# Two of the eight Wout pieces converted inside the last feed-forward, and block 0's products behind block 1

## The chip, the cores and the metric

The kernel runs on one core of a Trainium2 chip. The metric is the device time of one execution in microseconds; lower is better. The core has TensorE (PE, with its weight loads shown as PEld), VectorE (DVE), ScalarE (ACT), GpSimd (POOL) and SyncE (SP), whose queue issues most DMAs. Each engine works through its own instructions in order, and waits on semaphores for the others.

## The reference

Three modules follow one another: an attention with a learned relative bias, a mixture of eight experts with one expert for each token, and a plain feed-forward. All inputs are float32. What matters here is the end of the second and all of the third:

```python
for e in range(E):                      # 8 experts, D = 512, F = 1024, 2304 tokens
    mask = expert_idx == e
    h = np.maximum(x[mask] @ w1[e], 0.0)
    out[mask] = gate_w[mask, None] * (h @ w2[e])
...
h = x @ w_in                            # 2304 x 512 @ 512 x 2048
r = np.maximum(h, 0.0)
g = r * r
return (g @ w_out).astype(np.float32)   # 2304 x 2048 @ 2048 x 512
```

w_in and w_out reach the kernel as 64-bit floating point words, seen as pairs of 32-bit halves.

## The kernel before

The kernel keeps float32 accuracy with float16 matmuls: each operand is split into a high and a low float16 half, and each product is made of three matmuls (high-high, high-low, low-high).

**Expert stage.** `run_slots(0, NMOST)` goes over 22 slots of 128 tokens of one expert. In each slot PE does ff1 in two halves (2 x 48 matmuls, L1220), eight or sixteen transposes (L1203) and ff2 (24 matmuls, L1235). Four slots ahead, SP loads the next expert's first weights (`load_slot`, L999, 2 MB), and one slot ahead, between the matmuls of ff2, its second weights (`load_w2`, L1008, vt<-wsc, 2 MB); both are skipped when the expert stays the same.

**Conversion.** Into the same slots goes the conversion of the third module's weights from 64-bit words to float16 halves: `convert(i)` handles one of 16 pieces, eight of w_in (kept in `wih`) and eight of w_out. A piece's steps are a 1 MB load (L1106 or L1109), an Abs on ACT (L1116), two tensor_scalars (L1118, L1119) and two shift steps (L1121, L1123) on DVE, for w_out four subtractions of 256 columns on POOL (L1136), a cast on ACT (L1140), a subtraction on DVE (L1142) and a store of 896 KB to `wosc` in DRAM (L1144). `pieces` writes the order of these steps out by hand, with loads three pieces ahead for the first ones and two ahead for the last four. `piece(t, n)` paces them: in quarter n of slot t the generator `conv` is called until

```python
while done[0] < (1 if t < 2 else 1 + (t - 2 + 0.25 * n) * CPACE):
```

no longer holds, with CPACE = 6.1 calls a slot. The w_out product uses a 2 x 2 scheme with seven products instead of eight (Strassen's, in Winograd's form), so POOL's subtractions make the seven weight combinations.

**Last feed-forward.** It begins when the expert stage is over. SP loads all eight w_out pieces from `wosc` into `woh` (L1505). Nine blocks of 256 tokens follow. `g_unit(j, c)` is one of eight units of a block: 24 matmuls into one of four PSUM buffers `pf1` (L1422), a relu on ACT into `gf` (L1428, two buffers of a pair of units each), and after each second unit a square (L1433, on ACT for blocks 0 and 1, on DVE later), four combinations on POOL (L1438), and then, for the pair before, `g_split`: a cast on ACT (L1445) and a subtraction on DVE (L1446), which write the float16 halves `g2`. `ff2_of(j)` is a generator with the seven products of a block, each of 24 matmuls over the eight pairs c of g2 and woh (L1460), with their scalings and sums on ACT and DVE and two scatters to the output. The loop at the end places them: in block j, products of block j - 1 are called ahead of units c > 2 (c > 4 in block 1), and what is left of them behind the block's last unit.

Pools wait for the tiles whose memory they take over; the order on each engine is the order in which the program writes the instructions.

Of the kernel before, what the change touches and what calls it, by code (L numbers as in the profile page):

```python
# [7 lines left out]
F32 = mybir.dt.float32  # L8
F16 = mybir.dt.float16
U32 = mybir.dt.uint32  # L10
I32 = mybir.dt.int32
AF = mybir.ActivationFunctionType
ALU = mybir.AluOpType
# [10 lines left out]
P = 128  # L24
# [14 lines left out]
W1S, W2S, YS = 64.0, 64.0, 2.0 ** -8  # L39
WIS, RS, WOS = 64.0, 2.0 ** -8, 64.0  # L40
OUTS = 2.0 ** -22
CPACE = 6.1
NCONV, NWIN = 16, 8
HSW = 134
TINY64, HUGE = 2.0 ** -15 * 1.125, 3e38

# [37 lines left out]
def body(ctx: ExitStack, tc: tile.TileContext, q, k, v, wsm, emb, tau, mw1, mw2, win, wout, cst_d, lsk_d, ids_d, out):  # L84
    nc = tc.nc
    win, wout = win.bitcast(U32), wout.bitcast(U32)
    PE, ACT, DVE, POOL, SP = nc.tensor, nc.scalar, nc.vector, nc.gpsimd, nc.sync
# [863 lines left out]
    with tc.manual_schedule():  # L951
# [231 lines left out]
        wrp = ep("e_wr", 1)  # L1183
# [77 lines left out]
            DVE.tensor_copy(orow[:, i:i + 1], yr[:, DM + 1:XW])  # L1261


        conv = pieces([convert(i, wrp) for i in range(NCONV)])
        done = [0]
        state = ["tail"]
        yq, yd = [], []
# [115 lines left out]
        with ExitStack() as fctx:  # L1383
            fp = lambda n, bufs, **kw: tp(fctx, n, bufs, **(kw if "space" in kw else dict(side="right")))
            woh = fp("f_wo", 1).tile([P, 8, 2, 7, 256], F16, name="woh")
            gp = fp("f_g", 2)
            gfp = fp("f_gf", 2)
            op_ = fp("f_o", 2)
            up = fp("f_u", 1)
            ysp2 = fp("f_ys", 2)  # L1390
            pf1 = fp("f_p1", 4, space=PSUM)
            pf2 = fp("f_p2", 1, space=PSUM)
            NB = NTILE // 2
            gts, gfs, late, outs = {}, {}, [], []
            yv = lambda j: y0[:, :, :, 256 * (j % 2):256 * (j % 2) + 256]

            def y_load(j):
                for i in range(2):
                    t = 2 * j + i
                    SP.dma_start(out=us_t[t % 4][:, :XW], in_=y_d[t * P:(t + 1) * P, :])  # L1400

            def y_split(t):
                y2, yr = yv(t // 2), us_t[t % 4]
                y_rows(t, yr)
                ysr = ysp2.tile([P, 2, 4, P], F16, name="ysr")
                y4 = yr[:, :DM].rearrange("p (k n) -> p k n", k=4)
                o = slice(t % 2 * P, t % 2 * P + P)
                ACT.copy(ysr[:, 0], y4)
                DVE.tensor_tensor(out=ysr[:, 1], in0=y4, in1=ysr[:, 0], op=ALU.subtract)
                for a in range(2):  # L1410
                    SP.dma_start_transpose(out=y2[:, a, :, o], in_=ysr[:, a].rearrange("p k n -> p (k n)"))

            def g_unit(j, c):
                y2 = yv(j)
                if c == 0:
                    gts[j] = gp.tile([P, 2, 7, 8, P], F16, name="g2")
                p_ = pf1.tile([P, 2, 256], F32, name="pf1")
                for h in range(2):
                    f, i = 8 * h + c, 0
                    for kc in range(4):  # L1420
                        for a, b in ((0, 0), (0, 1), (1, 0)):
                            PE.matmul(p_[:, h], lhsT=wih[:, a, kc, f * P:(f + 1) * P], rhs=y2[:, b, kc, :],  # L1422
                                      start=(i == 0), stop=(i == 11))
                            i += 1
                if c % 2 == 0:
                    gfs[j] = gfp.tile([P, 8, 2, P], F32, name="gf")
                g = gfs[j]
                ACT.activation(g[:, 0:4, c % 2, :], p_.rearrange("p h (i n) -> p (h i) n", i=2), AF.Relu, scale=RS)  # L1428
                if c % 2 == 0:
                    return  # L1430
                g4 = g[:, 0:4].rearrange("p q c n -> p (q c n)")
                if j < 2:
                    ACT.activation(g4, g4, AF.Square)  # L1433
                else:
                    DVE.tensor_tensor(out=g4, in0=g4, in1=g4, op=ALU.mult)  # L1435
                for d, x, y, op in ((4, 0, 2, ALU.add), (5, 4, 1, ALU.subtract), (6, 1, 0, ALU.subtract),
                                    (7, 3, 5, ALU.subtract)):
                    POOL.tensor_tensor(out=g[:, d], in0=g[:, x], in1=g[:, y], op=op)  # L1438
                g_split()
                late.append((g, gts[j], c - 1))  # L1440

            def g_split():
                while late:
                    g, gt, c = late.pop()
                    ACT.copy(gt[:, 0, :, c:c + 2, :], g[:, 1:8])  # L1445
                    DVE.tensor_tensor(out=gt[:, 1, :, c:c + 2, :], in0=g[:, 1:8], in1=gt[:, 0, :, c:c + 2, :], op=ALU.subtract)  # L1446

            def ff2_of(j):
                gt = gts.pop(j)
                m = [meta[:, 2 * j + i, 0:1] for i in range(2)]  # L1450
                bank = [pf2.tile([P, 512], F32, name=f"pf2_{x}")[:, :256] for x in "abcd"]
                pa, pb, pc, pd = bank
                o = [op_.tile([P, DM], F32, name=f"o{i}") for i in range(2)]
                u = lambda nm: up.tile([P, 256], F32, name=nm)

                def prod(ps, s, w, first, end):
                    i = 0
                    for c in range(8):
                        for a, b in ((0, 0), (0, 1), (1, 0)):
                            PE.matmul(ps, lhsT=gt[:, a, s, c, :], rhs=woh[:, c, b, w, :],  # L1460
                                      start=(i == 0 and first), stop=(i == 23 and end), skip_group_check=True)
                            i += 1

                def comb(dst, ps, i, x):
                    DVE.scalar_tensor_tensor(out=dst, in0=ps, scalar=m[i], in1=x, op0=ALU.mult, op1=ALU.add)

                def put(i):
                    t = 2 * j + i
                    w = POOL.indirect_dma_start(out=out, out_offset=bass.IndirectOffsetOnAxis(ap=orow[:, t:t + 1], axis=0),  # L1469
                                                in_=o[i], in_offset=None, bounds_check=NT - 1, oob_is_err=False).ins  # L1470
                    for other in outs:
                        tc.declare_no_dep(w, other, reason="disjoint rows")
                    outs.append(w)

                prod(pa, 0, 0, True, False)
                s = [u(f"s{i}") for i in range(2)]
                for i in range(2):
                    ACT.activation(s[i], pa, AF.Copy, scale=m[i])
                yield
                prod(pb, 4, 4, True, True)  # L1480
                u2 = [u(f"u{i}") for i in range(2)]
                for i in range(2):
                    comb(u2[i], pb, i, s[i])
                yield
                prod(pc, 3, 3, True, False)
                u4 = u("u4")
                comb(u4, pc, 0, u2[0])
                yield
                prod(pd, 5, 5, True, False)
                comb(o[0][:, 256:], pd, 0, u4)  # L1490
                yield
                prod(pa, 2, 2, False, True)
                ACT.activation(o[1][:, :256], pa, AF.Copy, scale=m[1])  # L1493
                yield
                prod(pc, 6, 1, False, True)
                comb(o[1][:, 256:], pc, 1, u2[1])
                put(1)
                yield
                prod(pd, 1, 6, False, True)
                comb(o[0][:, :256], pd, 0, u2[0])  # L1500
                put(0)
                yield

            for g in range(8):
                SP.dma_start(out=woh[:, g].rearrange("p a q n -> p (a q n)"), in_=wosc[:, g * 3584:(g + 1) * 3584])  # L1505
            for j in range(NB):
                two = ff2_of(j - 1) if j else iter(())
                last = j == NB - 1
                for c in range(8):
                    if c > (2 if j > 1 else 4) and not (last and c == 6):  # L1510
                        next(two, None)
                    g_unit(j, c)
                    if 0 < j < NB - 1:
                        if c == 0:
                            y_load(j + 1)
                        if c in (3, 5):
                            y_split(2 * (j + 1) + c // 2 - 1)
                if last:
                    g_split()
                for _ in two:  # L1520
                    pass
            for _ in ff2_of(NB - 1):
                pass
# [66 lines left out]
```

## Time and the profile before

| what | value |
|---|---|
| median of 3 runs | 1011.57 us (1011.03 to 1012.91) |
| profiled execution | 1017.84 us, span 1016.0 us |
| PE busy in the span | 947.2 us (93%) |
| DVE, ACT, POOL busy | 662.3, 540.9, 497.0 us |
| granted PE clock, mean | 0.982 |
| expert stage, first to last ff2 | 404 to 648 us |
| last feed-forward | 650 to 1005 us |

The span runs from the first to the last instruction of the profiled execution; what is outside it (1.8 us) is start and end. Busy time of an engine is the time in which it executes an instruction; idle time is put down to what released the engine.

### The profile page before, as it was taken

Reading aid. Unit: us, or ns where it says so; the run is one execution under the profiler, and the core shown is the slowest. Engines: PE = TensorE matmul, PEld = TensorE weight load, DVE = VectorE, ACT = ScalarE, POOL = GpSimd, SP = SyncE. Lnnn points to the kernel's source line nnn. Section 1 sums busy time; section 2 is a strip of 40 time slices with the busy share of each in tenths; the row PEclk is TensorE's granted clock in tenths of the full one; section 3 lists DMA queues with packets and bytes.
Section 4 is the critical chain, followed back from the end, with each engine's and each line's share of the span. In section 5 each row is a group of like instructions: output and inputs, shape, how many; then the busy total and the mean of one; then the engine's idle time right before and its main releaser. Section 6 shows DMA issues by size and latency. Waiting matters only on the chain. (4 is left out here: it accounts for less than half of the span.)

```text
span 1016.0 us, 24944 instructions
## 1 busy us (share of the span) xinstructions
PE 947.2 (93%) x9725; PEld 749.5 (74%) x9725; DVE 662.3 (65%) x1229; ACT 540.9 (53%) x1000; POOL 497.0 (49%) x415
## 2 busy tenths in 40 slices
PE   8687999999899879999989999999999999999995
PEld 4456776677577658777657667688888888888884
DVE  6665999988988664677866867245445455545441
ACT  6666777777777574455756665255323333333330
POOL 1213536437433352456637787266454554645541
PEclk9798999999999999999999999999999999999998
DMA  9988985998779343698898574362111111111001
GB/s 299 329 242 265 327 276 174 303 267 265 242 228 326 137 125 108 229 336 300 336 410 318 196 271 170 143 275 50 25 53 43 32 52 43 32 53 22 22 1 42
DMA packets 78844, 187.18 MB, mean 184 GB/s; under 512 B 26648, under 2 KB 26776, under 8 KB 76128
## 3 DMA queue, kind: packets, MB, share of 16 engines
q1 hardware_dynamic: 72656, 169.98, 50.1%
q0 software_dynamic: 6064, 15.54, 4.6%
q8 instruction: 78, 1.28, 0.6%
q14 instruction: 46, 0.38, 0.1%
HBM read 171.65 MB, written 51.73 MB: 220 GB/s over the span
## 5 line engine op out<-in xcount | busy, mean ns | idle before, releaser
L1438 POOL TENSOR_TENSOR gf<-gf 128x256 f32<-128x256 f32 x144 | 165.9, 1171 | 146.5 <-DVE gf L1435 124.5
L1422 PE MATMUL pf<-big,wih 128*128 128x256 f16 x1728 | 196.0, 273 | 1.7 <-PEq L1376 1.7
L1422 PEld LDWEIGHTS <-wih 128*128 128x128 f16 x1728 | 169.0, 98 | 21.6 <-issue 2.1
L1460 PEld LDWEIGHTS <-g 128*128 128x128 f16 x1512 | 147.4, 98 | 18.7 <-issue 1.0
L1428 ACT ACTIVATE gf<-pf 128x512 f32<-128x512 f32 x72 | 42.5, 597 | 193.5 <-PE pf L1422 135.7
L1220 PE MATMUL ph<-x,w1b 128*128 128x128 f16 x2112 | 125.6, 219 | 4.6 <-ACT x L1204 2.4
L1220 PEld LDWEIGHTS <-w1b 128*128 128x128 f16 x2112 | 120.6, 98 | 9.5 <-issue 4.4
L471 POOL TENSOR_TENSOR wh<-wr,w2s_c 128x1024 f16<-128x1024 f32 x32 | 61.4, 1918 | 132.4 <-DMA wr<-in_mw_dram 83.1
L1235 PE MATMUL py<-vt,h 128*128 128x512 f16 x528 | 119.0, 382 | 6.1 <-DMA vt<-wsc 6.1
L1446 DVE TENSOR_TENSOR g<-gf,g 128x1792 f16<-128x1792 f32 x36 | 85.5, 2375 | 50.2 <-ACT g L1445 50.2
L522 ACT ACTIVATE pr<-ssb,mn 128x576 f32<-128x576 f32 x144 | 111.8, 777 | 11.9 <-DVE mn L509 11.7
L509 DVE CUSTOM_DVE_ANT_0 ssb<-ps_s,bias 128x576 f32<-128x576 f32 x144 | 107.5, 749 | 4.6 <-DMA bias<-bias_d 2.5
L498 PE MATMUL ps_s<-kst,qd 128*128 128x288 f16 (+1 forms) x640 | 96.4, 291 | 14.0 <-DVE mn L509 9.5
L1435 DVE TENSOR_TENSOR gf<-gf 128x1024 f32<-128x1024 f32 x28 | 34.3, 1225 | 113.6 <-ACT gf L1428 113.6
L1235 PEld LDWEIGHTS <-h 128*128 128x128 f16 x528 | 51.1, 98 | 65.0 <-issue 8.6
L531 PE MATMUL ps_t<-cst,pr 128*128 128x128 f32 x576 | 92.7, 284 | 1.3 <-DVE pt L209 0.6
L556 PE MATMUL pv<-pt,vt 128*64 128x128 f32 (+1 forms) x1280 | 85.1, 276 | 8.0 <-DMA vt<-in_v_dram 5.7
L556 PEld LDWEIGHTS pv<-pt,vt 128*64 128x64 f32 x1280 | 67.6, 141 | 24.4 <-issue 18.2
L531 PEld LDWEIGHTS ps_t<-cst,pr 128*128 128x128 f32 x576 | 65.3, 145 | 24.8 <-issue 19.7
L498 PEld LDWEIGHTS <-qd 128*128 128x128 f16 (+1 forms) x640 | 56.4, 101 | 29.1 <-issue 18.5
L207 ACT COPY pt<-ps_t 128x512 f32<-128x512 f32 x99 | 57.1, 577 | 14.9 <-PE ps_t L531 11.0
L1445 ACT CAST g<-gf 128x1792 f16<-128x1792 f32 x36 | 60.3, 1676 | 4.3 <-POOL gf L1438 4.3
(194 smaller groups left out, 1547.8 us busy)
## 6 DMA issues: line engine op xcount, KB each, us to landing
vt<-wsc SPq DMA_DIRECT2D x88, 512.0 KB
wr<-in_mw_dram SPq DMA_DIRECT2D x76, 512.0 KB
kst<-in_mw_dram SPq DMA_DIRECT2D x44, 512.0 KB
wsc<-wh SPq DMA_DIRECT2D x32, 512.0 KB
bias<-bias_d SPq DMA_DIRECT2D x16, 576.0 KB
bias_d<-rt SPq DMA_DIRECT2D x28, 295.5 KB
qd<-qh SPq DMA_DIRECT2D x64, 128.0 KB
wr<-in_win_dram SPq DMA_DIRECT2D x8, 1024.0 KB
```

The source lines that it names most:

```text
L471: POOL.tensor_tensor(out=wh[:, 0], in0=wr, in1=w2s_c.to_broadcast([P, 1024]), op=ALU.mult)
L498: PE.matmul(s[r, hf, :288], lhsT=qd[:, h2, i, pr, r], rhs=kst[x - x % 2][:, pr, h2, x % 2, js], start=(i == 0), stop=(i == 1))
L509: DVE.tensor_tensor_reduce(out=ss.rearrange("p (a j) -> p a j", a=2), in0=s[:, :, :288], in1=btile[bkey[u]][:, h2].rearrange("p (a j) -> p ...
L522: ACT.activation(pr_sb[k_ // 2][:, h2], ssb.pop(k_), AF.Exp, bias=mns.pop(k_), scale=-1.0, accum_out=sums[c, b][:, h:h + 1])
L531: PE.transpose(pt_ps[k_][:, jc * P:(jc + 1) * P], src[:, j0:j0 + P], eye)
L556: PE.matmul(pv[o, cs], lhsT=vb[:, 2 * jc + h2, d] if jc < 4 else vb[o, 8, d], rhs=a[h2][:, jc, cs] if jc < 4 else e[o, cs], start=(jc == 0 ...
L1220: PE.matmul(p_[:, f4, :], lhsT=w[:, a, kc, f * P:(f + 1) * P], rhs=x2[:, b, kc, :], start=(i == 0), stop=(i == 11))
L1235: PE.matmul(p_, lhsT=h2[:, a, fc, :], rhs=wb2[fc // 2][:, b, fc % 2, :], start=(i == 0), stop=(i == 23))
L1422: PE.matmul(p_[:, h], lhsT=wih[:, a, kc, f * P:(f + 1) * P], rhs=y2[:, b, kc, :], start=(i == 0), stop=(i == 11))
L1438: POOL.tensor_tensor(out=g[:, d], in0=g[:, x], in1=g[:, y], op=op)
L1446: DVE.tensor_tensor(out=gt[:, 1, :, c:c + 2, :], in0=g[:, 1:8], in1=gt[:, 0, :, c:c + 2, :], op=ALU.subtract)
L1460: PE.matmul(ps, lhsT=gt[:, a, s, c, :], rhs=woh[:, c, b, w, :], start=(i == 0 and first), stop=(i == 23 and end), skip_group_check=True)
```

## The change

Only 14 of the 16 pieces are converted in the expert stage, at 5.4 calls a slot. The raw rows of the last two w_out pieces are loaded at the start of the last feed-forward into the memory of block 1's `g2` tile, before that tile gets its own contents. `finish(i)` does the same steps on them as `convert` (its scratch lies in that tile too) and writes the halves straight into `woh[:, 6]` and `woh[:, 7]`. The dictionary `ORDER` says after which units (8 j + c) of blocks 0 and 1 each next step is emitted. The six other pieces come from `wosc` as before. g2's dimensions are put in another order, so that a pair of units fills one contiguous quarter of the tile. Block 0's seven products no longer stand between units of block 1, but all behind its last unit.

```diff
-CPACE = 6.1
-NCONV, NWIN = 16, 8
+CPACE = 5.4
+NCONV, NWIN, NLATE = 16, 8, 2
...
-        conv = pieces([convert(i, wrp) for i in range(NCONV)])
+        conv = pieces([convert(i, wrp) for i in range(NCONV - NLATE)])
...
-                if c == 0:
-                    gts[j] = gp.tile([P, 2, 7, 8, P], F16, name="g2")
+                if c == 0 and j not in gts:
+                    gts[j] = gp.tile([P, 4, 2, 7, 2, P], F16, name="g2")
...
-                    ACT.copy(gt[:, 0, :, c:c + 2, :], g[:, 1:8])
-                    DVE.tensor_tensor(out=gt[:, 1, :, c:c + 2, :], in0=g[:, 1:8], in1=gt[:, 0, :, c:c + 2, :], op=ALU.subtract)
+                    ACT.copy(gt[:, c // 2, 0], g[:, 1:8])
+                    DVE.tensor_tensor(out=gt[:, c // 2, 1], in0=g[:, 1:8], in1=gt[:, c // 2, 0], op=ALU.subtract)
...
-                            PE.matmul(ps, lhsT=gt[:, a, s, c, :], rhs=woh[:, c, b, w, :],
+                            PE.matmul(ps, lhsT=gt[:, c // 2, a, s, c % 2, :], rhs=woh[:, c, b, w, :],
...
-            for g in range(8):
+            for j in range(2):
+                gts[j] = gp.tile([P, 4, 2, 7, 2, P], F16, name="g2")
+            spare = gts[1].rearrange("p d a q c n -> p (d a q c n)").bitcast(U32)
+            rows = [spare[:, :2048], spare[:, 3072:5120]]
+            flat = spare[:, 5120:7168].bitcast(F32)
+            bits = [spare[:, 6144:7168], spare[:, 2048:3072]]
+            for i in range(NLATE):
+                g = 8 - NLATE + i
+                SP.dma_start(out=rows[i], in_=wout[g * P:(g + 1) * P, :])
+
+            def finish(i):
+                wr = rows[i].rearrange("p (n t) -> p n t", t=2)
+                lo, hi = wr[:, :, 0], wr[:, :, 1]
+                tb = flat.rearrange("p (q n) -> p q n", q=8)
+                af, b = flat[:, :1024], bits[i]
+                bf = b.bitcast(F32)
+                ACT.activation(bf, hi.bitcast(F32), AF.Abs)
+                yield
+                DVE.tensor_scalar(bf, bf, TINY64, None, op0=ALU.max)
+                DVE.tensor_scalar(b, b, 3, 0x3FFFFFF8, op0=ALU.logical_shift_left, op1=ALU.bitwise_and)
+                yield
+                DVE.scalar_tensor_tensor(out=b, in0=lo, scalar=29, in1=b, op0=ALU.logical_shift_right, op1=ALU.bitwise_or)
+                yield
+                DVE.scalar_tensor_tensor(out=af.bitcast(U32), in0=hi, scalar=0xC0000000, in1=b,
+                                         op0=ALU.bitwise_and, op1=ALU.bitwise_or)
+                yield
+                for d, x, y in ((4, 0, 1), (5, 2, 4), (6, 2, 0), (7, 3, 5)):
+                    POOL.tensor_tensor(out=tb[:, d], in0=tb[:, x], in1=tb[:, y], op=ALU.subtract)
+                yield
+                dh, dl = (woh[:, 8 - NLATE + i, a].rearrange("p q n -> p (q n)") for a in range(2))
+                ACT.activation(dh, flat[:, 256:], AF.Copy, scale=WOS)
+                yield
+                DVE.scalar_tensor_tensor(out=dl, in0=flat[:, 256:], scalar=WOS, in1=dh, op0=ALU.mult, op1=ALU.subtract)
+                yield
+
+            ends = [finish(i) for i in range(NLATE)]
+            ORDER = {3: (0,), 4: (0,), 5: (0, 0), 6: (0, 1), 7: (1,), 8: (0, 1), 9: (0,), 10: (1, 1), 12: (1,), 13: (1,)}
+
+            for g in range(8 - NLATE):
...
-                    if c > (2 if j > 1 else 4) and not (last and c == 6):
+                    if j > 1 and c > 2 and not (last and c == 6):
                         next(two, None)
                     g_unit(j, c)
+                    for i in ORDER.get(8 * j + c, ()):
+                        next(ends[i])
```

## Rows read from the trace of the kernel before

**Rows 1.** Windows, two stages: start and end, busy us of each engine (instructions), clock, DMA.

```profile
404.06:649.98 245.92, 234.65 (x2639) 169.56 (x2636) 175.30 (x237) 139.18 (x173) 154.44 (x138) 0.99 0.75 278
649.98:1004.60 354.62, 353.82 (x3240) 316.35 (x3240) 166.81 (x159) 126.41 (x157) 183.51 (x162) 1.00 0.19 56
```

**Rows 2.** PE's waits, 404 to 650 us: us in total, times, longest.

```profile
PE py L1235 <- DMA vt<-wsc: 6.1, 3, 3.4
...
PE ph L1220 <- ACT x L1204: 1.3, 2, 1.0
...
PE ph L1220 <- DVE w1b L1015: 1.0, 2, 0.6
```

**Rows 3.** PE in order of time, expert stage: start, us, operation, idle before.

```profile
485.25 5.34 PE L1235 MATMUL py<-vt,h 128*128 128x512 f16 x24 [2.42 <-DMA vt<-wsc]
...
522.24 6.75 PE L1235 MATMUL py<-vt,h 128*128 128x512 f16 x24 [3.39 <-DMA vt<-wsc]
```

**Rows 4.** Window of the expert stage, up to slot 10's product.

```profile
508.00:522.00 14.00, 10.53 (x126) 7.80 (x124) 9.48 (x11) 9.16 (x13) 7.99 (x8) 0.99 1.02 413
```

**Rows 5.** SP's queue in order of time, slot 9.

```profile
506.99 0.41 SPq L1109 DMA_DIRECT2D wr<-in_wout_dram  x1
508.71 4.69 SPq L1008 DMA_DIRECT2D vt<-wsc  x4
```

**Rows 6.** Groups by line, 404 to 650 us: the conversion's steps (busy us, mean ns).

```profile
L1136 POOL TENSOR_TENSOR tb<-tb 128x256 f32<-128x256 f32 x32 | 26.1, 835 | 12.9 <-DVE tb L1123 6.3 <-DVE ys L1244 5.9
...
L1121 DVE SCALAR_TENSOR_TENSOR tb<-wr,tb 128x1024 uint32<-128x1024 uint32 x16 | 20.0, 1252 | 1.1 <-DVEq L1024 0.8 <-DMA vt<-wsc 0.2
...
L1116 ACT ACTIVATE tb<-wr 128x1024 f32<-128x1024 f32 x16 | 18.5, 1157 | 17.3 <-DVE wr L1142 6.9 <-DVE wih L1131 3.9 <-issue 3.4
L1142 DVE SCALAR_TENSOR_TENSOR wr<-tb,wr 128x1792 f16<-128x1792 f32 x8 | 16.1, 2018 | 5.1 <-ACT wr L1140 5.1
...
L1140 ACT ACTIVATE wr<-tb 128x1792 f16<-128x1792 f32 x8 | 13.6, 1695 | 11.5 <-POOL tb L1136 10.8 <-DVE tb L1119 0.7
...
L1118 DVE TENSOR_SCALAR tb<-tb 128x1024 f32<-128x1024 f32 x16 | 13.0, 815 | 2.3 <-DVEq L1024 2.0
```

**Rows 7.** ACT in order of time, blocks 0 and 1.

```profile
673.05 1.08 ACT L1428 ACTIVATE gf<-pf 128x512 f32<-128x512 f32 x2 [2.69 <-DVE g L1446]
...
681.58 1.67 ACT L1445 CAST g<-gf 128x1792 f16<-128x1792 f32 x1
685.94 1.08 ACT L1428 ACTIVATE gf<-pf 128x512 f32<-128x512 f32 x2 [2.69 <-DVE g L1446]
```

**Rows 8.** PE in order of time, blocks 0 and 1.

```profile
649.98 34.22 PE L1422 MATMUL pf<-big,wih 128*128 128x256 f16 x312 [1.66 <-PEq L1376]
684.03 2.78 PE L1460 MATMUL pf_a<-woh,g 128*128 128x256 f16 x24
686.65 2.78 PE L1422 MATMUL pf<-big,wih 128*128 128x256 f16 x24
...
710.23 5.95 PE L1422 MATMUL pf<-big,wih 128*128 128x256 f16 x53
```

**Rows 9.** POOL in order of time, blocks 0 and 1.

```profile
657.19 2.89 POOL L1438 TENSOR_TENSOR gf<-gf 128x256 f32<-128x256 f32 x4 [5.55 <-ACT gf L1433]
...
675.30 4.68 POOL L1438 TENSOR_TENSOR gf<-gf 128x256 f32<-128x256 f32 x4 [1.76 <-ACT gf L1433]
```

**Rows 10.** DVE in order of time, blocks 0 and 1.

```profile
676.83 2.57 DVE L1446 TENSOR_TENSOR g<-gf,g 128x1792 f16<-128x1792 f32 x1 [3.88 <-ACT g L1445]
...
696.89 2.57 DVE L1446 TENSOR_TENSOR g<-gf,g 128x1792 f16<-128x1792 f32 x1 [3.33 <-ACT g L1445]
```

**Rows 11.** SP's queue at the start of the last feed-forward.

```profile
656.45 5.62 SPq L1505 DMA_DIRECT2D woh<-wosc  x8
```

**Rows 12.** Windows around slot 10's product.

```profile
519.00:520.00 1.00, 0.00 (x0) 0.00 (x0) 0.69 (x1) 1.00 (x2) 0.00 (x0) 1.00 1.04 393
522.00:525.00 3.00, 2.77 (x7) 1.01 (x7) 2.75 (x4) 1.19 (x2) 1.97 (x2) 0.50 1.02 410
```

## The prediction

> **What bounds the kernel now.** I read the busy times by stage first [rows 1]. The reader is to see two stages that are both filled by TensorE: the expert stage, 245.9 us with 234.7 us of it busy, and the last feed-forward, 354.6 us with 353.8 us busy. In the second there is nothing to win: its PE work is 9 blocks of 15 groups of 24 matmuls, and only lost PE time can change its length. In the first, the waits of PE say what could be won [rows 2]: 6.1 us for the loads of the second expert weights (vt<-wsc), 2.3 us for ACT and DVE (1.3 and 1.0); in the order of time the two large ones are 2.42 us ahead of slot 7's product and 3.39 us ahead of slot 10's, and that last product then ran 6.75 us where slot 7's took 5.34 [rows 3], 1.4 us more. So all gaps of the stage that loads and conversion could cause are 6.1 + 2.3 + 1.4 = 9.8 us.
>
> **Part 1, the pace (16 pieces at 6.1 become 14 at 5.4).** In the 14 us up to slot 10's product the DMA engines are 102% busy and move 413 GB/s [rows 4]: here the transfers set the pace, and each MB ahead of slot 10's weights makes them later by 1.05 MB / 413 GB/s = 2.5 us. A call number k of the conversion runs in the first quarter slot above 2 + (k - 2)/CPACE. The load of piece 9 is call 45: 43/6.1 = 7.05 puts it into slot 9.25, and the queue view shows it at 506.99, just ahead of slot 10's weights at 508.71 [rows 5]. With 5.4, 43/5.4 = 7.96, it goes to slot 10.0, behind them. Of five loads (calls 17, 24, 31, 38, 45) four stay ahead: 2.5 us of the 3.39 go, and about 0.9 is left, less than the 2.42 after which the clock stayed up [rows 3], so the 1.4 us go too. The load of piece 6 moves the other way, from slot 5.75 (ahead of slot 9's raw weights) to 6.25 (behind them, ahead of slot 7's second weights): the 2.42 us can grow by the head start that is lost (I take 2 us, about the time of its own 1 MB, less than the 2.5 us above), but what is lost there is transferred in the meantime, so that the sum up to slot 10 stays. Of the 2.3 us behind ACT and DVE I take a third, 0.8, since a slot has 11% fewer steps. Gain 2.5 + 1.4 + 0.8 = 4.7 us; bounds: a loss of 1 us (piece 6 costs 2 that come back only in part), and all of 9.8.
>
> **Part 2, the conversion inside blocks 0 and 1.** Two pieces bring, each, an ACT Abs (1.16), two DVE tensor_scalars (0.81 for the first), two DVE shift steps (1.25 each), four POOL subtractions (0.84 each), an ACT cast (1.70) and a last DVE subtraction (2.02) [rows 6]. The sums would fit in the idle time of the three engines; the question is what stands behind each step in its queue. Now the elementwise work of a pair of units is a chain: two relus, square, cast of the pair before, subtraction of the pair before, and only then the next relus, because there are two gf buffers. It takes 6.45 us a pair (two pairs from 673.05 to 685.94 [rows 7]) where PE needs 2 x 2.62 = 5.24 (684.03 to 686.65 [rows 8]). PE does not feel that yet: four PSUM buffers let it run ahead, and unit 14 would need unit 10's relu (685.94 + 0.6) when PE comes to it at 649.98 + 14 x 2.62 = 686.7. There is no slack left at that point even without conversion. POOL has little room too: its four operations of a pair take 2.89 us alone and 4.68 us beside a DVE subtraction of 2.57 [rows 9, 10].
>
> Into this chain go, by the written order: the Abs of the second piece between relus 6 and 7, which run back to back (+1.16); the cast of the first piece between relus 8 and 9 (+1.70); and the first piece's POOL work ahead of pair 3's. It starts when DVE has done two shift steps behind the subtraction that ends at 672.95 (676.83 - 3.88 [rows 10]), at 675.5, and runs until about 679.7 (2.9 alone, 4.7 beside DVE); pair 3's four then last until about 685.3, beside 2.9 us of DVE steps, where its cast would have come at 681.58 + 1.16 + 1.70 = 684.4: +0.9. Together the chain is 3.7 us late: relu 10 begins at about 689.6, unit 14 at 690.2 instead of 686.7, unit 15 ends at about 695.5.
>
> The end of the second piece decides. DVE's last step of piece one and the second shift step of piece two follow the subtraction of pair 3 at 689.6: 691.8, 693.0. Piece two's POOL work stands beside pair 4's subtraction and the split of y: 5.9 us, to 698.9. ACT has relu 12 at 696.1 and then waits for it: cast to 700.6, relu 13 and square to 702.2, cast of pair 5 to 703.9, subtraction of pair 5 to 706.4, and behind that, in DVE's queue, piece two's last subtraction, to 708.8.
>
> **Part 3, block 0's products behind block 1.** Now three of seven lie between units, from 684.03 on, and block 2 begins at 710.23 [rows 8]. The order alone costs PE nothing: 16 units and 7 products end at 710.2 either way. But the first product goes through all eight weight pieces, and its 23rd matmul reads the low half of piece 8. Without a wait it would run at 649.98 + 16 x 2.62 + 22 x 0.109 = 694.3; by part 2 it waits until 708.8. The loss is 14.5 us (the 3.5 us ahead of unit 14 lie inside it, since the end of the chain sets the resume). Bounds: were the chain not lengthened at all, the last step would still follow the subtraction that now ends at 696.89 + 2.57 = 699.46 [rows 10] and end at 701.5, a loss of 7.2; were the raw rows some 4 us late as well, because their loads come as late as the woh loads do now (656.45 [rows 11]) and share the engines with them, and POOL stretched by 2 us more, it would be 715, a loss of 20.7. I take 14.5, since the 6.45 us chain of now fits the same stretched durations.
>
> **The clock.** After 3.39 us without a matmul the granted clock went from 1.00 to 0.50, that is 2.4 to 1.2 GHz, and stayed there for 2.8 us after the restart at 522.24 [rows 12]; this was worth 1.4 us [rows 3]. A wait of 11 us in block 0's first product should do that too: +1.4, once. The Trainium skill, page "TensorE: Matmul & The Clock Gate", section "Part 1: The HAM clock gate", says the same in general: the slow clock is the default, and sustained activity releases it. The trace agrees at slot 10; by that rule the sum is the one below, and without it 1.4 us less.
>
> **Part 4, what costs nothing.** Two direct loads of 1 MB replace two round trips through wosc; they are issued at the start of the stage, and the DMA share there leaves room (0.19 over the stage [rows 1]). The new order of g2's dimensions keeps every operand's size. The steps' scratch lies in g2 of block 1, whose first quarter is written only at unit 11, after the first piece's raw rows were read. If that cover fails, it is the upper bound above.
>
> **Sum.** -4.7 + 14.5 + 1.4 = +11.2 us. The profiled execution took 1017.8 us (span 1016.0), 6.3 more than the median of the runs, 1011.6; I put the difference on the median: 1022.8 us.
>
> **Rivals.** (a) The chain keeps its pace: the steps fall into idle time (ACT 2.69, DVE 3.88, POOL 1.76 us a pair [rows 7, 9, 10]), and only the last subtraction's place costs: 7.2 + 1.4 - 4.7 = +3.9, 1015.5 us. For it: the sums fit. Against: Abs and cast stand between relus that run back to back. (b) Faster: with the products gone from the queues the chain runs ahead of now (relu 13 no longer waits behind two scalings), and piece two ends at 698.0: loss 3.7, no clock fall worth counting, -4.7 + 3.7 = -1.0, or 1010.6; it decides from an end before 699.0. Against: now's own subtraction of pair 5 ends at 699.46, and the last step is queued behind it. (c) Dearer: late rows and a second fall of the clock, 20.7 + 2.8 - 4.7 = +18.8, 1030.4, and up to 1036 if the expert stage gives nothing. (d) The expert stage gives all 9.8: with 15.9 in the other stage still +6.1, 1017.7; it lies inside my range.
>
> **How the numbers follow.** Forecast, with (d), 0.62, own range 1016 to 1029; (a) 0.12; (c) 0.10; (b) 0.11; about no change 0.05 (the measurement tells 0.2%, 2 us, from none). Leaving out the outer part of (c) and most of (b), the range is 1011 to 1030. Faster 0.11, same 0.05, slower 0.62 + 0.12 + 0.10 = 0.84.
>
> **What would show it.** Right: in block 0's first product a PE wait of 8 to 13 us, released by DVE's last subtraction of the second piece (or ACT's cast just before), a half-speed clock behind it, 2 to 4 us ahead of unit 14 released by ACT; in the expert stage less waiting for vt<-wsc, above all at slot 10. Wrong: PE without a gap between 650 and 725; a wait of ACT's Abs for the rows; or an expert stage as long as before or longer.

## The result and the profile after

The changed kernel takes 1021.71 us (median of 10 runs, 1014.77 to 1025.69) against 1011.63 us of the kernel before on the same chip (10 runs): ratio 1.008, 95% interval 1.0054 to 1.0106. It is slower by about 0.8%, some 8 to 10 us; the prediction was 1022.8 us. The profiled execution of the changed kernel took 1024.84 us, 7.0 more than that of the kernel before.

The profile says where. From the first matmul of slot 0's ff2 to the first matmul of the last feed-forward the changed kernel needs 640.53 - 403.58 = 236.95 us, the kernel before 245.92 [rows 1]: 9.0 us less. From there to the first matmul of block 2 it needs 717.30 - 640.53 = 76.77 us, the kernel before 710.23 - 649.98 = 60.25 [rows 8]: 16.5 us more. From there to the start of the last product both need the same 291.85 us (717.30 to 1009.15 and 710.23 to 1002.08).

PE of the changed kernel in order of time, blocks 0 and 1 (start, us, operation, idle before and what ended it); it answers to [rows 8]:

```profile
640.53 36.84 PE L1422 MATMUL pf<-big,wih 128*128 128x256 f16 x336 [0.43 <-PEq L1376]
680.64 6.88 PE L1422 MATMUL pf<-big,wih 128*128 128x256 f16 x48 [3.27 <-ACT gf L1428]
687.36 2.46 PE L1460 MATMUL pf_a<-woh,g 128*128 128x256 f16 x21
690.50 0.27 PE L1460 MATMUL pf_a<-woh,g 128*128 128x256 f16 x1 [0.69 <-ACT woh L1534]
698.71 0.58 PE L1460 MATMUL pf_a<-woh,g 128*128 128x256 f16 x2 [7.94 <-DVE woh L1536]
699.09 5.28 PE L1460 MATMUL pf_b<-woh,g 128*128 128x256 f16 x24
...
717.30 8.02 PE L1422 MATMUL pf<-big,wih 128*128 128x256 f16 x72
```

The 16 units run as one stretch up to unit 13; ahead of unit 14 PE stands 3.27 us for a relu. Block 0's first product gets through 21 matmuls, waits 0.69 us for the high half of the last weight piece, piece 8, and 7.94 us for its low half, and the product behind the wait takes 5.28 us instead of 2.78. Units 14 and 15 took 6.88 us instead of 5.40 (48 matmuls). The clock is the reason for both long ones; windows of the changed kernel (start and end, length, busy us of PE, PEld, DVE, ACT, POOL, then PE clock, DMA share, GB/s):

```profile
680.00:682.00 2.00, 1.36 (x7) 0.96 (x7) 2.00 (x1) 1.97 (x3) 0.48 (x1) 0.57 0.00 0
682.00:684.00 2.00, 2.00 (x13) 1.42 (x12) 1.81 (x3) 2.00 (x3) 0.30 (x1) 0.57 0.00 0
...
694.00:698.00 4.00, 0.00 (x0) 0.00 (x0) 4.00 (x2) 1.80 (x4) 2.77 (x2) 0.50 0.17 33
699.00:702.00 3.00, 3.00 (x16) 2.07 (x15) 2.88 (x4) 1.77 (x3) 2.92 (x3) 0.50 0.23 44
```

It is at or near its lower level, 1.2 GHz, after each of the two gaps. ACT in order of time, answering to [rows 7]:

```profile
663.62 0.60 ACT L1428 ACTIVATE gf<-pf 128x512 f32<-128x512 f32 x1 [2.70 <-DVE g L1446]
664.12 1.16 ACT L1520 ACTIVATE g<-g 128x1024 f32<-128x1024 f32 x1
665.18 0.58 ACT L1428 ACTIVATE gf<-pf 128x512 f32<-128x512 f32 x1
...
675.88 1.69 ACT L1445 CAST g<-gf 128x1792 f16<-128x1792 f32 x1 [1.35 <-POOL gf L1438]
...
688.75 1.70 ACT L1534 ACTIVATE woh<-g 128x1792 f16<-128x1792 f32 x1 [1.75 <-POOL g L1531]
```

The two late pieces, the seventh and eighth of w_out, are called piece 7 and piece 8 from here on. Abs of piece 8 stands between relus 6 and 7 (663.62 and 665.18). The cast of pair 3 at 675.88 had waited 1.35 us for POOL, and the cast of piece 8 at 688.75 had waited 1.75 us for POOL; both waits are in the forecast. POOL's rows, answering to [rows 9]:

```profile
659.43 4.69 POOL L1438 TENSOR_TENSOR gf<-gf 128x256 f32<-128x256 f32 x4 [1.76 <-ACT gf L1433]
666.53 4.69 POOL L1531 TENSOR_TENSOR g<-g 128x256 f32<-128x256 f32 x4 [2.42 <-DVE g L1527]
671.18 9.30 POOL L1438 TENSOR_TENSOR gf<-gf 128x256 f32<-128x256 f32 x8
683.70 5.02 POOL L1531 TENSOR_TENSOR g<-g 128x256 f32<-128x256 f32 x4 [3.22 <-DVE g L1527]
688.68 2.90 POOL L1438 TENSOR_TENSOR gf<-gf 128x256 f32<-128x256 f32 x4
```

From 666.53 to 680.48 POOL is never idle: four subtractions of piece 7 (4.69 us) and then the eight operations of pairs 3 and 4 (9.30). And DVE's, answering to [rows 10]:

```profile
693.63 2.56 DVE L1446 TENSOR_TENSOR g<-gf,g 128x1792 f16<-128x1792 f32 x1 [5.50 <-ACT g L1445]
696.12 2.54 DVE L1536 SCALAR_TENSOR_TENSOR woh<-g,woh 128x1792 f16<-128x1792 f32 x1
```

The last step of piece 8 stands behind the subtraction of pair 5 and ends at 698.66; PE goes on at 698.71.

In the expert stage the two waits of [rows 3] look like this in the changed kernel:

```profile
480.91 1.46 PE L1235 MATMUL py<-vt,h 128*128 128x512 f16 x6 [0.26 <-DMA vt<-wsc]
482.52 4.04 PE L1235 MATMUL py<-vt,h 128*128 128x512 f16 x18 [0.16 <-DMA vt<-wsc]
...
516.73 6.87 PE L1235 MATMUL py<-vt,h 128*128 128x512 f16 x24 [2.39 <-DMA vt<-wsc]
```

Slot 7's product waits 0.42 us instead of 2.42, slot 10's 2.39 instead of 3.39, and slot 10's still runs at the low clock (6.87 us). PE's other waits of [rows 2], 1.3 us for ACT and 1.0 us for DVE, are gone.

### The profile page after: what moved, and what is told of

Its sections match the earlier page's. It is cut to its first block, busy times and chain, and to the rows that moved or that the text cites. A ratio compares the mean times of both kernels' runs of the same rounds, so it can differ in the third digit from the quotient of the medians.

```text
span 1023.1 us, 24938 instructions
## 1 busy us (share of the span) xinstructions
PE 949.2 (93%) x9725; PEld 750.8 (73%) x9725; DVE 657.3 (64%) x1229; ACT 542.1 (53%) x1000; POOL 500.2 (49%) x415
## 5 line engine op out<-in xcount | busy, mean ns | idle before, releaser
L1445 ACT CAST g<-gf 128x1792 f16<-128x1792 f32 x36 | 60.3, 1676 | 5.7 <-POOL gf L1438 5.7
```

## The experiments

All ratios are against the kernel before on the same chip in the same series, with their 95% intervals; between series the chip differs (the kernel before had medians of 1020.1, 1015.0, 1018.5 and 1018.1 us in the four), so runs of different series are compared by the lengths of their stages. These come from one profile each, "expert" from the first ff2 matmul to the first matmul of the last feed-forward, "blocks 0, 1" from there to block 2's first matmul. In single profiles the expert stage of one and the same code differs: with 14 pieces at 5.4 it took 235.2 to 240.2 us in nine of them, so a difference of a few us between two profiles of that stage proves little by itself. The three with the loads and steps of 6.1 calls (kernel before, runs 1 and 3) lie closer, 245.4 to 245.9.

| run | ratio | expert, us | blocks 0, 1, us |
|---|---|---|---|
| kernel before | 1 | 245.9 | 60.3 |
| changed kernel | 1.0080 (1.0054 to 1.0106) | 237.0 | 76.8 |
| the same again, with the third series | 1.0098 (1.0063 to 1.0133) | 239.5 | 75.6 |
| 1 order of block 0's products alone | 1.0011 (0.9976 to 1.0045) | 245.7 | 61.7 |
| 2 14 pieces at 5.4, two left out | 0.9926 (0.9892 to 0.9960) | 238.6 | 60.3 |
| 3 14 pieces at 6.1, two left out | 0.9984 (0.9952 to 1.0015) | 245.4 | 60.3 |
| 4 changed, ACT's steps moved | 1.0129 (1.0077 to 1.0181) | 240.2 | 75.8 |
| 5 changed, piece 8 last | 0.9963 (0.9927 to 0.9999) | 237.9 | 69.6 |
| 6 changed, subtractions on DVE, new order | 0.9962 (0.9931 to 0.9993) | 238.3 | 67.2 |
| 7 both of 5 and 6 | 0.9938 (0.9905 to 0.9971) | 235.2 | 64.6 |
| 8 before, loads two calls later | 0.9959 (0.9926 to 0.9993) | 242.8 | 60.6 |
| 9 one late piece | 1.0039 (1.0007 to 1.0070) | 252.1 | 61.1 |
| 10 changed, subtractions on DVE alone | 1.0102 (1.0057 to 1.0147) | 237.9 | 77.7 |
| 11 run 7, scalings first | 1.0014 (0.9983 to 1.0045) | 238.2 | 66.8 |

### 1. The order of block 0's products alone

```diff
-                    if c > (2 if j > 1 else 4) and not (last and c == 6):
+                    if j > 1 and c > 2 and not (last and c == 6):
```

> The kernel before, with one part of the change alone: all seven products of block 0 behind the last unit of block 1; nothing of the conversion is moved. Theory (the order costs nothing, the wait for the last weight piece does): same time as before within 0.2%, 0 us; in blocks 0 and 1 PE has no gap over 0.5 us, because relu 10 ends at 686.55 in the profile before and unit 14 comes at 686.7. Rival (the units run too far ahead of the elementwise chain once no products lie between them): a gap of 2 us or more ahead of unit 14 or 15, released by ACT, and some 2 to 4 us more.

Same time, within the noise. PE in order of time, in this kernel:

```profile
652.63 42.08 PE L1422 MATMUL pf<-big,wih 128*128 128x256 f16 x384 [1.12 <-PEq L1376]
...
706.01 2.78 PE L1460 MATMUL pf_a<-woh,g 128*128 128x256 f16 x24 [0.82 <-ACT s L1478]
709.05 2.78 PE L1460 MATMUL pf_c<-woh,g 128*128 128x256 f16 x24 [0.26 <-DVE u L1465]
```

All 16 units run without a gap. There are 0.82 us and 0.26 us of waiting later, for block 0's own scalings and sums, which now follow the cast and subtraction of pair 6. The first of them is over the 0.5 us that was expected. The rival, a gap ahead of unit 14 or 15, is out, with 1.4 us more in blocks 0 and 1 than before (61.7 against 60.3) as what the order does cost.

### 2 and 3. The expert stage alone, at both paces

The kernel before with 14 pieces in the expert stage; pieces 7 and 8 of Wout are not converted, and pieces 1 and 2 are loaded in their place (run 3 has the same edit with CPACE left at 6.1):

```diff
-CPACE = 6.1
+CPACE = 5.4
...
-        conv = pieces([convert(i, wrp) for i in range(NCONV)])
+        conv = pieces([convert(i, wrp) for i in range(NCONV - NLATE)])
...
-                SP.dma_start(out=woh[:, g].rearrange("p a q n -> p (a q n)"), in_=wosc[:, g * 3584:(g + 1) * 3584])
+                SP.dma_start(out=woh[:, g].rearrange("p a q n -> p (a q n)"), in_=wosc[:, g % 6 * 3584:(g % 6 + 1) * 3584])
```

> The kernel before with 14 pieces at 5.4 calls a slot and nothing else: two of the eight Wout pieces are not converted at all, and in their place woh gets pieces 0 and 1 a second time, so the output is not the reference's. It measures what the expert stage alone gains. The profile after shows 9.0 us less from slot 0's ff2 to the first matmul of the last feed-forward (236.95 against 245.92); the prediction had 4.7. Theory: 5 to 9 us faster, waits for vt<-wsc well under the 6.1 us of before. Rival (the 9.0 us are mostly a difference between two executions, not of the change): 0 to 2 us faster.

> As the run with 14 pieces in the expert stage alone (two Wout pieces left out, pieces 0 and 1 loaded twice), but at the old 6.1 calls a slot: every load of the first twelve pieces keeps its slot, and the conversion ends about two and a half slots earlier. Theory (the gain comes from loads that move behind slot 10's weights, by the slower pace): the waits for vt<-wsc stay at 5 to 6 us and the half-speed product at slot 10 stays, gain 0 to 3 us. Rival (fewer bytes and steps as such give the gain): as fast as the 5.4 run within 2 us.

14 pieces at 5.4 are 0.74% faster (7.5 us), 14 pieces at 6.1 are not faster beyond the noise. So removing two pieces at the old pace gives nothing that can be measured; going to 5.4 as well does. The slower pace moves both the loads and the other steps, and these two runs do not part them. PE's waits in the expert stage of the run at 5.4 (us in total, times, longest):

```profile
PE py L1235 <- DMA vt<-wsc: 2.5, 2, 1.6
PE ph L1220 <- issue: 2.4, 6, 0.5
```

and of the run at 6.1:

```profile
PE py L1235 <- DMA vt<-wsc: 4.8, 2, 3.0
PE ph L1220 <- ACT x L1204: 2.0, 2, 1.0
PE px L1203 <- POOL xs L1038: 1.5, 3, 0.7
...
PE ph L1220 <- DVE w1b L1015: 1.0, 2, 0.6
```

At 6.1 the weights are late by 4.8 us, and ACT, POOL and DVE hold PE for 2.0 + 1.5 + 1.0 us more; at 5.4 the first is halved and the others are gone. The theory that only loads matter is too narrow: 2.3 us of the 6.9 between the two stages are theirs. Nor did the half-speed product at slot 10 stay at 6.1, as the theory had it; in run 3 that product waited 1.72 us and took 5.60:

```profile
525.75 5.60 PE L1235 MATMUL py<-vt,h 128*128 128x512 f16 x24 [1.72 <-DMA vt<-wsc]
```

In run 1, whose expert stage is that of the kernel before, it waited 1.22 + 0.28 us. The 3.39 us of [rows 3] are what one execution showed.

### 4. ACT's steps out from between back-to-back relus

```diff
-            ORDER = {3: (0,), 4: (0,), 5: (0, 0), 6: (0, 1), 7: (1,), 8: (0, 1), 9: (0,), 10: (1, 1), 12: (1,), 13: (1,)}
+            ORDER = {3: (0,), 4: (0,), 5: (0, 0, 1), 6: (0,), 7: (1,), 8: (1,), 9: (0, 0), 10: (1, 1), 13: (1, 1)}
```

> The changed kernel with another written order of the same conversion steps: ACT's Abs of the second piece behind unit 5 and both casts behind units 9 and 13, where ACT waits for DVE's subtraction anyway, and no ACT step between two relus that run back to back. Theory (steps between back-to-back relus lengthen the chain): the gap of 3.27 us ahead of unit 14 falls below 0.7, DVE's last subtraction of the second piece ends 3 to 5 us earlier, counted from the first matmul of the stage, and the wait of block 0's first product, 8.6 us now, stays above 5 because that step still stands behind the subtraction of pair 5; time 3 to 5 us under the changed kernel, about 1017. Rival (POOL's doubled work, not ACT, holds the chain): the gap ahead of unit 14 stays at 2 us or more and the time within 1 us of the changed kernel.

The theory falls. The ratio is not below that of the changed kernel (1.0129 against 1.0080 and 1.0098, with overlapping intervals), and the gap ahead of unit 14 is what it was, on PE:

```profile
683.01 7.07 PE L1422 MATMUL pf<-big,wih 128*128 128x256 f16 x48 [3.27 <-ACT gf L1428]
```

because on ACT the cast of pair 3 now waits 3.65 us for POOL and starts as late as before, 678.24 - 642.90 = 35.34 us after the stage's first matmul (675.88 - 640.53 = 35.35 in the changed kernel):

```profile
678.24 1.69 ACT L1445 CAST g<-gf 128x1792 f16<-128x1792 f32 x1 [3.65 <-POOL gf L1438]
```

### 10 and 6. POOL's subtractions on DVE, alone and with a new order

Run 10 has the first edit, run 6 both:

```diff
-                    POOL.tensor_tensor(out=tb[:, d], in0=tb[:, x], in1=tb[:, y], op=ALU.subtract)
+                    DVE.tensor_tensor(out=tb[:, d], in0=tb[:, x], in1=tb[:, y], op=ALU.subtract)
...
-            ORDER = {3: (0,), 4: (0,), 5: (0, 0), 6: (0, 1), 7: (1,), 8: (0, 1), 9: (0,), 10: (1, 1), 12: (1,), 13: (1,)}
+            ORDER = {3: (0,), 4: (0, 0), 5: (1,), 6: (0, 0), 7: (0,), 8: (0, 1), 10: (1, 1, 1), 11: (1,), 12: (1,)}
```

> The changed kernel with one edit: the four subtractions of each late piece on DVE instead of POOL, the written order of the steps as it is. If POOL alone lengthens the chain, the gap of 3.27 us ahead of unit 14 falls below 0.7, as in the run with both edits (0.60). If the chain is as late as the later of two delays, POOL's second load or ACT's 1.16 + 1.70 us between back-to-back relus, taking one away leaves the other: 2 to 3 us stay. Moving ACT's steps alone had left 3.27.

> The changed kernel with the four subtractions of a late piece on DVE instead of POOL, and the steps written so that each stands where its engine waits: no ACT step between back-to-back relus, the last step of the second piece behind unit 12, ahead of the subtraction of pair 5. New theory after the run with the steps moved on ACT alone (POOL's second load, not ACT's, holds the chain): the cast of pair 3 no longer waits for POOL for over 1 us, the gap ahead of unit 14 falls from 3.27 to 1 us or less, and the wait for piece 8 from 8.6 to 4 to 6; 4 to 7 us under the changed kernel, 1 to 4 above the kernel before. Rival (any step more in this stretch lengthens the chain by its own time, whichever engine does it): the gap stays at 3 us.

Alone, the move leaves a gap of 2.62 us ahead of unit 14 (and 0.74 ahead of unit 12):

```profile
675.68 5.40 PE L1422 MATMUL pf<-big,wih 128*128 128x256 f16 x48 [0.74 <-ACT gf L1428]
683.71 7.07 PE L1422 MATMUL pf<-big,wih 128*128 128x256 f16 x48 [2.62 <-ACT gf L1428]
...
702.52 0.59 PE L1460 MATMUL pf_a<-woh,g 128*128 128x256 f16 x2 [7.94 <-DVE woh L1536]
```

Run 10 does not show ACT's steps alone, though, because the subtractions now delay DVE. The cast of pair 2 ended at 671.23, but its subtraction on DVE began only at 672.40, behind those of piece 7:

```profile
669.30 3.18 DVE L1531 TENSOR_TENSOR g<-g 128x256 f32<-128x256 f32 x4
672.40 2.54 DVE L1446 TENSOR_TENSOR g<-gf,g 128x1792 f16<-128x1792 f32 x1
```

So 1.2 us of the chain's delay there are DVE's new load. The rest, 2.62 + 0.74 - 1.2 = 2.2 us, is an estimate of what ACT's steps would hold alone.

With both edits, 0.60 us are left, and the wait for piece 8's low half is 2.90 instead of 7.94, less than the 4 to 6 expected:

```profile
674.89 5.40 PE L1422 MATMUL pf<-big,wih 128*128 128x256 f16 x48 [0.60 <-ACT gf L1428]
...
685.90 0.59 PE L1460 MATMUL pf_a<-woh,g 128*128 128x256 f16 x2 [2.90 <-DVE woh L1536]
```

So POOL's second load holds the chain by 3.3 us by itself (run 4), and beside it, not on top of it, stand ACT's steps between relus with some 2 us. Taking away either leaves a gap; run 6, which takes away both, closes most of it. Its new order also moves DVE's steps of both pieces, so the 0.60 is the work of the whole order and not of two edits alone. That the last step of piece 8 now stands ahead of pair 5's subtraction shortens the wait for it further.

### 5 and 7. Piece 8 last in block 0's first four products

```diff
-                def prod(ps, s, w, first, end):
-                    i = 0
-                    for c in range(8):
+                def prod(ps, s, w, first, end, cs=range(8)):
+                    i = 3 * cs[0]
+                    for c in cs:
...
-                prod(pa, 0, 0, True, False)
+                cs = range(8)
+                if j == 0:
+                    for ps, x, end in ((pa, 0, False), (pb, 4, True), (pc, 3, False), (pd, 5, False)):
+                        prod(ps, x, x, True, end, range(7))
+                    cs = range(7, 8)
+                prod(pa, 0, 0, True, False, cs)
...
```

The first calls for pb, pc and pd get the same `cs`.

> The changed kernel, in block 0's products alone: the first four of them run over weight pieces 1 to 7 first, and their matmuls on piece 8 follow behind all four. Theory (of the 16.5 us lost in the last feed-forward most is the wait for piece 8 and the slow clock behind it): 3 x 21 matmuls of 0.109 us, 6.9 us, cover the 8.6 us wait, about 1.7 us of it stay, and the half-speed stretch behind it goes; from the first matmul of the stage to block 2's first unit 8 to 10 us less than the 76.8 of the changed kernel, time equal to the kernel before within 2 us. Rival (something else behind the wait holds block 0's products, the sums on ACT and DVE): the gap comes back further on, less than 4 us won.

> Both edits together: the late pieces' subtractions on DVE in the new order, and block 0's first four products with piece 8 last. Theory: the wait for piece 8 is covered wholly (6.9 us of cover against 4 to 6), the gap ahead of unit 14 is 1 us or less, so the last feed-forward is as long as before within 1.5 us and the whole gain of the expert stage is left, 0.993 of the kernel before (the run with 14 pieces alone had 0.9926). Rival: the two edits win the same time twice, and the sum stays at 0.998 or above.

In run 5, on the changed kernel, blocks 0 and 1 are 7.2 us shorter (69.6 against 76.8), a little less than expected. The wait shrinks to 2.12 us, but the clock falls here too (0.50 granted from 701.00 to 703.00), and one product takes 4.20 us:

```profile
699.13 0.38 PE L1460 MATMUL pf_a<-woh,g 128*128 128x256 f16 x2 [2.12 <-DVE woh L1541]
...
701.24 4.20 PE L1460 MATMUL pf_a<-woh,g 128*128 128x256 f16 x24 [0.75 <-ACT s L1483]
```

In run 7 there is no wait for piece 8 any more, but one of 2.99 us for the scalings of the first product, which stand in ACT's queue behind the cast of pair 6:

```profile
674.21 5.40 PE L1422 MATMUL pf<-big,wih 128*128 128x256 f16 x48 [0.60 <-ACT gf L1428]
...
693.09 2.78 PE L1460 MATMUL pf_a<-woh,g 128*128 128x256 f16 x24 [2.99 <-ACT s L1483]
```

So blocks 0 and 1 take 4.3 us more than before, not 1.5 as expected, and the ratio, 0.9938, is still the lowest of the versions that do all the work, though its interval overlaps those of runs 5, 6 and 8.

### 11. The scalings ahead of the cast

Run 7 with the first product's scalings written ahead of pair 6's cast and subtraction.

> The fastest version so far (two late pieces with their subtractions on DVE and steps where engines wait, piece 8 last in block 0's first products), with ACT's two scalings of block 0's first product ahead of the cast of pair 6 instead of behind it. In that version PE waits 2.99 us for these scalings. Theory: the wait falls below 0.5 us, the last feed-forward is within 1.5 us of the kernel before, and the time 0.990 to 0.993 of it. Rival (DVE's sums, next in the queue behind pair 6's subtraction, hold the products instead): the wait moves to DVE u, and the time stays at 0.994.

```profile
697.84 2.78 PE L1461 MATMUL pf_a<-woh,g 128*128 128x256 f16 x24 [1.42 <-ACT s L1484]
703.15 4.27 PE L1461 MATMUL pf_c<-woh,g 128*128 128x256 f16 x24 [2.54 <-DVE u L1466]
```

The rival's mechanism holds: 1.42 us for the scalings stay, 2.54 us for DVE's sums come, and the product behind them ran at the low clock (4.27 us). It won nothing: blocks 0 and 1 take 66.8 us against 64.6, and the ratio is 1.0014, not the 0.994 that the rival had. The expert stage, which the edit does not touch, was 3.0 us longer in this profile (238.2 against 235.2); what else made the ratio worse is not shown.

### 8. The loads alone, 16 pieces

```diff
                 next(c, None)
-                if 0 < n <= NWIN and n + 3 < len(cs):
-                    next(cs[n + 3])
                 yield
                 next(d, None)
                 yield
                 next(c, None)
+                if 0 < n <= NWIN and n + 3 < len(cs):
+                    next(cs[n + 3])
                 yield
```

> The kernel before (16 pieces, 6.1 calls a slot, nothing in the last feed-forward), with one edit: the loads of pieces 5 to 12 stand two calls later in the written order, so that piece 9's falls into slot 9.5, behind slot 10's weights, instead of 9.25. Theory (the expert stage gains by where the loads stand, not by fewer pieces): 3 to 7 us faster, less waiting for vt<-wsc than the 4 to 6 us of the kernel before. Rival (the wider spacing of all steps is what gains): the same as before within 2 us.

```profile
PE px L1203 <- POOL xs L1038: 3.7, 3, 2.7
PE py L1235 <- DMA vt<-wsc: 2.1, 2, 1.3
PE ph L1220 <- ACT x L1204: 2.0, 2, 1.0
PE ph L1220 <- DVE w1b L1015: 1.0, 2, 0.6
```

4.2 us faster by the ratio, with all 16 pieces in the expert stage. The weights' waits fall to 2.1 us from 6.1. Those for ACT and DVE stay, 2.0 + 1.0, and 3.7 us of waits for POOL stand beside them (none in the kernel before, 1.3 and 1.5 in runs 1 and 3); the stage is 3.1 us shorter in the profile. So placing the loads gives a part of the gain. That the wider spacing of the other steps gives the rest follows from this and from runs 2 and 3 by subtraction; no run moved those steps alone. By the ratios, two moved lines in the kernel before won 0.41%, where run 7 won 0.62% with all its edits; the intervals overlap.

### 9. One late piece

15 pieces at 5.75, one late piece with DVE subtractions, block 0's products between the units as before.

> One late piece instead of two (15 pieces at 5.75 calls a slot, which still puts piece 9's load into slot 9.5, behind slot 10's weights), its subtractions on DVE, its steps at units 3, 4, 4, 6, 6, 7, 8, and block 0's products between the units of block 1 as in the kernel before. Theory: the expert stage keeps most of what 14 pieces won (4 to 8 us), the late piece is ready some 10 us before the first product, and the last feed-forward is as long as before within 1 us; 0.992 to 0.996 of the kernel before. Rival (the gain of the expert stage falls with the number of pieces that stay in it): 0.997 or above.

The last feed-forward costs 0.8 us, as expected, but the ratio, 1.0039, lies where the rival had it. The expert stage is 6 us longer than before:

```profile
PE px L1203 <- POOL xs L1038: 5.5, 2, 5.0
PE ph L1220 <- ACT x L1204: 3.7, 2, 2.1
PE py L1235 <- DMA vt<-wsc: 1.6, 2, 1.2
```

PE waits only 1.6 us for the weights. The largest wait is one of 5.01 us for POOL's split of the token rows (xs, L1038). Ahead of that split POOL had stood idle for 10.57 us, by the profile until a load of expert weights (wr<-in_mw_dram) had landed, and no step of the conversion ran on it in that time. The same idle time was 10.78 us in the kernel before and 10.39 us in the changed kernel, where PE did not wait for POOL in this place. The gain of the stage does not follow the pace or the number of pieces in a smooth way; with the written order of the loads as it was, only 5.4 of the three paces (6.1, 5.75, 5.4) gained. Why 5.75 is this bad stays open.

### The changed kernel again

> The changed kernel as it is, on the chip of these runs, as their base: 1.008 of the kernel before, the gap of 3.3 us ahead of unit 14 and some 8 us of waiting for piece 8 again.

1.0098, 75.6 us in blocks 0 and 1, a gap of 3.25 us ahead of unit 14 and 7.93 us for piece 8's low half: the loss repeats.

## Why the prediction was right, step by step

**Part 1, the pace.** Forecast -4.7 us, by 2.5 at slot 10, 1.4 of clock and 0.8 of ACT and DVE. In the two profiles it was -9.0; nine profiles of kernels with this expert stage (the changed kernel twice, runs 2, 4 to 7, 10 and 11) lie between 235.2 and 240.2 us, 238.1 in the mean, against 245.9 and 245.7, so -7.7. The side is right, but the term is too small and was made up of the wrong parts. Slot 10 gave 1.0 instead of 2.5 and kept the low clock; slot 7, of which I expected a loss if anything, gave 2.0; the 2.3 us for ACT and DVE went wholly and not by a third, and of the 1.66 us at the end of the stage [rows 8], which I had not counted, 0.43 are left. The 3.9 us that I expected at slot 10 came from one execution. Over the three profiles at 6.1 calls (kernel before, runs 1 and 3) that product waited 3.39, 1.50 and 1.72 us, over the nine at 5.4 it waited 0.58 to 2.81 and 1.9 in the mean, so little was won there; slot 7's wait fell from 2.4, 2.3 and 3.0 us to 1.1 in the mean; and no profile of the nine has a wait for ACT's x or for DVE's w1b. What I called the cause, loads behind slot 10's weights, gives a part (run 8), and nothing measurable comes from the smaller number of pieces at the old pace (run 3).

**Part 2, the chain.** Forecast: unit 14 3.5 us late, measured 3.27. The steps came in the forecast order and nearly at the forecast times: pair 3's cast behind POOL at 685.3 - 649.98 = 35.3 us after the stage's first matmul (measured 675.88 - 640.53 = 35.35), relu 10 at 39.6 (679.99 - 640.53 = 39.46). What misleads is the form of the sum, ACT's 1.16 + 1.70 us and then 0.9 us of POOL. The chain follows the later of two paths, and POOL's was the later one: without ACT's steps between relus the cast waits 3.65 us for POOL instead of 1.35 and starts at the same time (run 4). ACT's path would be late by some 2 us alone, by the estimate at run 10. The last step of piece 8 was to end 58.8 us after the stage's first matmul (708.8 - 649.98); it ended at 698.66 - 640.53 = 58.1.

**Part 3, the wait.** Forecast 14.5 us, with an 11 us wait in the first product behind a 3.5 us gap; measured 0.69 + 7.94 us behind 3.27 us. The wait was shorter since units 14 and 15 ran at the low clock and PE came later to a point whose end was set by DVE. By its end the loss is 58.1 - 44.3 = 13.8 us. Run 1 shows that the order of the products alone costs next to nothing, run 5 that covering the wait gives back 7 us.

**The clock.** Forecast one fall, +1.4 us; there were two. The first (6.88 us instead of 5.40) lies inside the wait and costs nothing more, the second cost 2.5 us (5.28 instead of 2.78). 13.8 + 2.5 = 16.3 of the 16.5 us.

**Part 4, nothing.** The two raw loads are issued at 648.23, 7.7 us after the stage's first matmul, and Abs of the first piece did not wait for them (it follows pair 0's cast at once); the cover held.

Of the rivals, (a), (b) and the late rows of (c) did not occur; the second fall of the clock in (c) did. (d), the whole 9.8 us in the expert stage, came near in the first profile (9.0 of 9.8), less so in the mean of the nine (7.7). The two stages missed by -4.3 and +0.6 us in that profile; that the sum of +11.2 is 1.1 us off the difference of the medians (10.1), and 4.2 off that of the two profiled executions (7.0), is in part luck.

## What to carry to other kernels

Work moved into a stage that another engine bounds is free only if the engine that does it keeps pace at every point of its queue: sum the chain from one buffer to its reuse, not the idle shares, and look at what the last moved step stands behind. Where two engines are late beside each other, undoing one shows little; undo both before the theory is dropped, and see that the edit does not load a third. And when a consumer must wait for one of eight pieces, it can do the other seven for several products first: here that took 7.2 us off blocks 0 and 1, hurrying the piece and its chain 9.6 (run 6), and both together 12.2 (run 7). A wait seen in one profile can be half as long in the next; a forecast that rests on it needs a second profile.

## What the runs showed of the hardware

The length of a gap alone did not tell whether the granted clock falls. After 2.39 us (changed kernel, slot 10) and 2.29 us (run 1, slot 7, whose product then took 7.03 us) it fell (granted 0.52 from 516.70 to 520.00, and 0.65 from 488.00 to 491.00); after 2.42 us (kernel before, slot 7 [rows 3]) and 3.03 us (run 3, slot 7: 5.34 us, granted 1.00 from 490.90 to 496.00) it did not. PE in order of time, run 1 and then run 3:

```profile
488.03 7.03 PE L1235 MATMUL py<-vt,h 128*128 128x512 f16 x24 [2.29 <-DMA vt<-wsc]
```

```profile
490.91 5.34 PE L1235 MATMUL py<-vt,h 128*128 128x512 f16 x24 [3.03 <-DMA vt<-wsc]
```

So the prediction's argument, that a wait below the 2.42 us after which the clock stayed up leaves it up, was not sound. What decides between these cases no run shows.

POOL's four operations of 128 x 256 on a pair take 2.90 us alone (648.29 in the changed kernel) and 4.69 us when DVE runs its subtraction of two inputs beside them (652.97), and eight in a row took 9.30 us in the changed kernel. The Trainium skill, page "GPSIMD Engine Reference", section "1. Specifications", says that GpSimd shares its SBUF interfaces with VectorE, with contention when a VectorE instruction has two SBUF inputs or runs in a 2-port mode; the trace agrees for two inputs, with these numbers. So moving work from POOL to DVE was no pure gain either: on DVE, in run 9, a late piece's four subtractions took 3.45 us beside POOL's eight operations of two pairs, which took 9.78.
